# The idle products at the head of a fused attention and mixture kernel: strided, backward and narrower operands in place of shifted ones

## The chip, the cores and the metric

The kernel runs on one core of one Trainium2 chip. The metric is the device time of one execution in microseconds (us). The kernel before took 1054.14 us, the median of three runs (1053.22 to 1054.45). The profile was taken from one further execution.

## What is computed

The first half is a gated linear attention. For each of 4 batches and 8 heads (dimension 48) a 48 x 48 state runs over 768 positions; its output, with the heads laid side by side, is a 3072 x 384 matrix `x`. The second half sends `x` through four experts and adds them up, weighted by normalised probabilities.

```python
for t in range(S):
    state = alpha[:, :, t, :, None] * state + np.einsum('bhd,bhe->bhde', k[:, :, t], v[:, :, t])
    y[:, :, t] = np.einsum('bhd,bhde->bhe', q[:, :, t], state)
...
p = domain_probs / (domain_probs.sum(-1, keepdims=True) + 1e-09)
for e in range(E):
    h = np.maximum(x @ w1[e], 0.0)
    out += p[:, e:e + 1] * (h @ w2[e])
```

Here S = 768, E = 4, `w1[e]` is 384 x 1024 and `w2[e]` is 1024 x 384.

## The kernel before, in words

The sequence is cut into 24 units of 128 positions (6 blocks for each of 4 batches). `attention(u)` (L280) is a Python generator that issues one unit in 17 steps, so that other work can be issued between the steps. Its steps are, in order: transpose alpha (`tp`, L277) and copy it out as `AT` (ACT, L288); transpose k and copy it as `KT` (L293); transpose q and multiply it by `AT` into `QT` (DVE, L307). Then come seven levels: for each, ACT copies a half of `QT` into a block `qb` (L328), DVE multiplies `QT`, the decay `dec` and `KT` (L335, L337, L348), and the second half of `KT` is copied by POOL in unit 0 and by ACT in all others (L347). The scores of levels 0 to 3 are small products `sc` (L355) which DVE takes over into `near` under a mask (L365). Later `far` (L410) and the scores of levels 4 and 5 follow, then two steps that copy `far` and `near` into `lat` (L423, L428), then the unit's result `yps` (L450), which ACT copies out as a part of `xT` (L467), and last the state (`sps`, L489).

The experts work on groups of units. The first group holds units 0 and 1; the others hold four. `up` (L531) makes the hidden rows (`one` and `two`, L562 and L570) and `down` (L623) multiplies them with `w2` (`ops`, L663). `advance` issues attention steps of later units between these products, after a plan that is worked out from costs written in the program, not from the chip.

Everything is issued in program order on each engine's queue (`tc.manual_schedule()`), and each queue is worked off in that order.

The change lies in the head, before the first `up`. There the only work is the attention of unit 0 and a few steps of unit 1. Between its steps the program issues products whose operands are zeros and whose output `idle` nobody reads. There are two kinds:

- `fill(n)` (L796) issues n products of 128 x 128 zeros in plain float32, from a part of a state tile. Each is two pairs of weight load and product in the trace. Seven of them (14 pairs) open the PE queue.
- `single(n)` (L819) takes n entries from the list `turns` and issues four products of each, with `float32r` operands from the zeroed tile `nothing` (128 x 2304 words): one pair each. The stationary operand (`held`, the weight load) is 128 columns; the moving one is 384 words (two entries have 512).

An entry of `turns` before is told by how far the moving operand starts from word 640 (`away`), its width, the number of stationary columns (one entry has 96), and its form: plain, `one_line` (the same two words repeated 192 times), `one_word` for the stationary operand, or `backwards` (step -1). The list has 17 entries, 68 products. They are issued in list order, in six places of the PE queue: 4 after the transposes of alpha, 4 after those of k, 28 after those of q, 8 after the scores of levels 0 to 3, 8 after the transposes of unit 1's k, and 16 after the last scores, right ahead of `yps`. The third group of eight holds the entry with 96 columns and the `one_line` entry; the last 16 are `one_word`, the two entries of 512 words, and `backwards`, in that order.

In the loop at L828 a pair (u, n) says: issue the next step of unit u, then n entries.

```python
for u, n in ((0, 1), (0, 1), (0, 1), (0, 2), (0, 2), (0, 1), (0, 1), (1, 0), (0, 0), (0, 1),
             (0, 1), (1, 1), (0, 1), (1, 0), (0, 0), (0, 2), (0, 2), (0, 0)):
    next(runs[u])
    single(n)
```

Of the kernel before, what the change touches and what calls it, by code (L numbers as in the profile page):

```python
# [20 lines left out]
def kernel(  # L21
# [37 lines left out]
    nc = tc.nc  # L59

    B, H, S, D = q.shape
    E, DM, F = moe_w1.shape
    P = 128
# [3 lines left out]
    QUAD = 32  # L67
# [3 lines left out]
    NT = B * P  # L71
# [13 lines left out]
    n = np.arange(QUAD)[None, :]  # L85
# [81 lines left out]
    def load(u, names):  # L167
        if u >= len(units):
            return
        cb, b = units[u]  # L170
        for nm in names:
            src = srcs[nm][b, :, cb * P:(cb + 1) * P, :].rearrange("h s d -> s h d")
            if nm != "v":
                nc.sync.dma_start(out=raw(u, nm)[:, :, :D], in_=src)
                continue

            pairs = raw(u, nm).rearrange("p (a i) d -> p a i d", i=2)
            src = src.rearrange("p (a i) d -> p a i d", i=2)
            nc.sync.dma_start(out=pairs[:, :, 0, :D], in_=src[:, :, 0])
            nc.sync.dma_start(out=pairs[:, :, 1, :TAIL], in_=src[:, :, 1, QUAD:])  # L180
            nc.sync.dma_start(out=pairs[:, :, 1, TAIL:D], in_=src[:, :, 1, :QUAD])
# [13 lines left out]
    def load_piece(l, i, beside=False):  # L195
        if i >= E * NQ * LAST:
            return
        gi, k = divmod(i, E * NQ)
        e, c = divmod(k, NQ)
        if gi > l:  # L200
            w = wt[l][i] = wts.tile([P, 3, KC * QF], F32R, name=f"w{l + 1}",
                                    bufs=AHEAD if l == 0 else NQ)
            nc.sync.dma_start(out=w.bitcast(F32), in_=kept[l][k])
            return
        if l == 1 and not beside:
            return
        if l == 0:

            if gi > 0 or e == 0:
                shared[c] = wts.tile([P, 3, KC * QF], F32R, name="w2", bufs=NQ)  # L210
            w = shared[c][:, 2 - e % 2 if gi == 0 else 2].bitcast(F32)
        else:

            place = (hidden[c][:, 0] if not split2(gi, e, c) else hidden[c + NQ // 2][:, 1])
            w = place.rearrange("p f n -> p (f n)")[:, :KC * QF].bitcast(F32)
        wt[l][i] = w
        if l == 0:
            heads = moe_w1[e].rearrange("(h d) f -> h d f", d=D)[:, :, c * QF:(c + 1) * QF]
            w = w.rearrange("p (c f) -> p c f", f=QF)
            for part in range(2):  # L220
                nc.sync.dma_start(out=w[:, part], in_=heads[part * H // 2:(part + 1) * H // 2, :QUAD])
            nc.sync.dma_start(out=w[:, 2], in_=heads[:, QUAD:])
        else:
            nc.sync.dma_start(
                out=w.rearrange("p (c d) -> p c d", d=DM),
                in_=moe_w2[e].rearrange("(c p) d -> p c d", p=P)[:, c * FPQ:(c + 1) * FPQ])
# [36 lines left out]
    def norm_probs():  # L263
        nc.vector.reduce_sum(out=tot, in_=p_all, axis=AX.X)
        nc.vector.tensor_scalar_add(out=tot, in0=tot, scalar1=1e-9)
        nc.vector.reciprocal(out=tot, in_=tot)
        nc.vector.tensor_mul(p_all, p_all, tot.unsqueeze(2).broadcast_to([P, NBLK, E]))
        nc.vector.tensor_scalar_mul(out=p_fine, in0=p_all, scalar1=FINE)
# [439 lines left out]
    def cost(layer, gi, e):  # L708
        n = len(groups[gi]) / 4
        if layer == 0:  # L710
            return 2.1 * n if split1(gi, e) else 2.6 * n
        return 4.1 if gi > 1 else 4.7 if split2(gi, e) else 5.4
# [56 lines left out]
    with tc.manual_schedule():  # L769
        nc.scalar.dma_start(out=ident_all, in_=nc.inline_tensor(ident_np, name="ident_c").ap())  # L770
        nc.scalar.dma_start(out=masks, in_=nc.inline_tensor(mask_np, name="masks_c").ap())
        nc.gpsimd.memset(sts[B - 1], 0.0)
        for nm in "akq":
            for r in (early[nm], apart[nm]):
                nc.gpsimd.memset(r[:, :, D:], 0.0)
        nc.gpsimd.memset(lat[HALF:, :, :HALF], 0.0)
        for t in values + blocks:
            nc.gpsimd.memset(t, 0.0)
        for t in sts[:-1]:
            nc.gpsimd.memset(t, 0.0)  # L780

        load(0, "akqv")
        load(1, "akqv")
        nc.sync.dma_start(out=p_all, in_=moe_domain_probs.rearrange("(n p) e -> p n e", p=P))
        for i in range(NQ):
            load_piece(0, i)

        idle = ps.tile([P, NT], F32, name="idle", tag="g", bufs=4)  # L790
        zeros = sts[B - 1].rearrange("p a i d -> p (a i d)")[:, :P]
        nothing = wts.tile([P, 3, KC * QF], F32R, name="w1", bufs=AHEAD)
        nothing = nothing.rearrange("p t n -> p (t n)")
        nc.vector.memset(nothing.bitcast(F32), 0.0)

        def fill(n):  # L796
            for _ in range(n):
                nc.tensor.matmul(idle[:, :P], lhsT=zeros, rhs=zeros, start=True, stop=True)

        def words(n, at):  # L800
            return nothing[:, at:at + n]

        def one_line(n, at):
            return words(2, at).unsqueeze(1).broadcast_to([P, n // 2, 2])

        def one_word(n, at):
            return words(1, at).broadcast_to([P, n])

        def backwards(n, at):
            return words(n, at)[:, ::-1]  # L810

        def turn(away=16, n=DM, m=P, moving=words, held=words, pair=2):
            return away, n, m, moving, held, pair

        turns = deque([turn(), turn(0), turn(8), turn(24), turn(32), turn(40), turn(48), turn(56),
                       turn(4), turn(12), turn(pair=1), turn(m=3 * QUAD), turn(moving=one_line),
                       turn(held=one_word), turn(8, NT), turn(48, NT), turn(moving=backwards)])

        def single(n):  # L819
            for _ in range(n):  # L820
                away, n, m, moving, held, pair = turns.popleft()
                for i in range(4):
                    nc.tensor.matmul(idle[:m, :n], lhsT=held(m, 256 * (i % pair)),  # L823
                                     rhs=moving(n, 640 + away), start=True, stop=True)

        runs = [attention(u) for u in range(len(groups[0]))]
        fill(7)
        for u, n in ((0, 1), (0, 1), (0, 1), (0, 2), (0, 2), (0, 1), (0, 1), (1, 0), (0, 0), (0, 1),  # L828
                     (0, 1), (1, 1), (0, 1), (1, 0), (0, 0), (0, 2), (0, 2), (0, 0)):
            next(runs[u])  # L830
            single(n)
        norm_probs()

        span = cost(0, 0, 0) * FCH / 2 + cost(1, 0, 0)
        waiting.extend((span * (k + 1) / 15, u, runs[u])
                       for k, u in enumerate([1, 1, 1, 0, 1, 0, *[1] * 8]))
        for fc in range(FCH):
            up(0, 0, fc, slice(0, 1))
            advance(cost(0, 0, 0) / 2)
        down(0, 0, [0], deque())  # L840
        while waiting:
            next(waiting.popleft()[2], None)
        clock = 0.0
        waiting.extend((1.0 + k, 1, runs[1]) for k in range(2))
        waiting.extend(deal())

        for (gi, e), after in zip(tasks, [*tasks[1:], (None, None)]):
            rest = gi == e == 0
            for fc in range(FCH):
                up(gi, e, fc, slice(1, len(groups[0])) if rest else None)  # L850
                advance(cost(0, gi, e) / (2 if rest else 1))
            each = len(groups[gi]) if split2(gi, e) else 1
            turns = [range(k, k + each) for k in range(rest, len(groups[gi]), each)]
            for k, slots in enumerate(turns):

                between = deque()
                if after[1] == 0:

                    for step, at in enumerate((0.0, 0.3, 0.42, 0.54) if gi == 0 else
                                              (0.0, 0.6, 0.7, 0.78)):  # L860
                        at = at * len(turns) - k
                        if 0 <= at < 1:
                            between.append((at, lambda step=step: split_x(after[0], step)))
                down(gi, e, slots, between)
        while stores:
            stores.popleft()()
# [28 lines left out]
```

## Time and profile before

| | |
|---|---|
| median of three runs | 1054.14 us |
| the profiled execution: its own time | 1053.91 us |
| its span, first to last instruction | 1052.1 us |
| what lies around the span | 1.8 us |
| PE busy, share of the span | 98% |
| DVE, ACT, POOL busy | 74%, 54%, 4% |
| PE idle products at L823 | 68, from 5.0 to 24.2 us |
| PE idle products at L798 | 14, from 1.2 to 3.9 us |
| first instruction of `yps` (L450) | 24.48 us |
| first instruction of `one` (L562) | 26.16 us |

The page of the profile gives the busy time of each engine, the span in slices, the chain of work that ended last and the costliest groups of instructions. A row of a group reads: line, engine, operation, output and inputs, shapes, count, busy time and mean time of one. [...]

### The profile page before, as it was taken

Reading aid. Unit: us, or ns where it says so; the run is one execution under the profiler, and the core shown is the slowest. Engines: PE = TensorE matmul, PEld = TensorE weight load, DVE = VectorE, ACT = ScalarE, POOL = GpSimd, SP = SyncE. Lnnn points to the kernel's source line nnn. Section 1 sums busy time; section 2 is a strip of 40 time slices with the busy share of each in tenths; the row PEclk is TensorE's granted clock in tenths of the full one; section 3 lists DMA queues with packets and bytes.
Section 4 is the critical chain, followed back from the end, with each engine's and each line's share of the span. In section 5 each row is a group of like instructions: output and inputs, shape, how many; then the busy total and the mean of one; then the engine's idle time right before and its main releaser. Section 6 shows DMA issues by size and latency. Waiting matters only on the chain.

```text
span 1052.1 us, 21692 instructions
## 1 busy us (share of the span) xinstructions
PE 1035.5 (98%) x8538; PEld 900.9 (86%) x8538; DVE 780.7 (74%) x1621; ACT 566.3 (54%) x1195; POOL 37.8 (4%) x81
## 2 busy tenths in 40 slices
PE   9899999999999999999999999999999999999998
PEld 8776777687787898898898998898989989898998
DVE  6488777668779868778877777986877875656565
ACT  4687876675757545446455435555474443323232
POOL 3010010000000000000000000000000000000000
PEclk9999999999999999999999999999999999999999
DMA  7596799997967949669669569576594454444531
GB/s 117 165 324 204 250 308 342 324 343 230 314 249 256 381 148 328 257 211 313 231 212 329 193 231 360 184 275 253 169 366 181 181 210 178 183 182 178 206 154 45
DMA packets 158549, 251.66 MB, mean 239 GB/s; under 512 B 120144, under 2 KB 134864, under 8 KB 135920
## 3 DMA queue, kind: packets, MB, share of 16 engines
q1 hardware_dynamic: 151984, 207.89, 58.5%
q0 software_dynamic: 6016, 42.08, 10.0%
q8 instruction: 67, 1.10, 0.4%
q10 hardware_dynamic: 448, 0.32, 0.1%
q14 instruction: 34, 0.28, 0.1%
HBM read 207.79 MB, written 42.47 MB: 238 GB/s over the span
## 4 chain that ended last, share of the span: by engine, by line
PE 87%; DVE 6%; ACT 4%; DMA 1%; issue 1%; POOL 0%; SPq 0%; ACTq 0%; DVEq 0%; POOLq 0%
PE ops L663 35%; PE one L570 23%; PE two L570 11%; PE sc L355 6%; PE yps L450 3%; PE tp L277 3%; PE one L562 2%; ACT qb L328 1%; PE sps L489 1%; PE idle L823 1%; PE far L410 1%; DMA hT<-in_moe_w_dram 1%; DVE near L365 1%; DVE hT L616 1%; DVE acc L692 1%
## 5 line engine op out<-in xcount | busy, mean ns | idle before, releaser
L663 PE MATMUL ops<-w,hT 128*128 128x384 f32 x1872 | 342.7, 339 | 0.2 <-DVE hT L616 0.2
L663 PEld LDWEIGHTS ops<-w,hT 128*128 128x128 f32 x1872 | 322.6, 188 | 4.0 <-ACT t L581 0.7
L570 PE MATMUL one<-xT,w 128*128 128x512 f32 x960 | 251.8, 398 | 1.3 <-DVE QT L335 0.9
L570 PEld LDWEIGHTS one<-xT,w 128*128 128x128 f32 x960 | 176.1, 188 | 39.2 <-DVE QT L335 1.5
L581 ACT ACTIVATE t<-one 128x512 f32<-128x512 f32 (+1 forms) x192 | 107.0, 557 | 175.8 <-PE one L570 170.6
L328 ACT COPY qb<-QT 64x256 f32<-64x256 f32 x336 | 136.6, 406 | 58.6 <-DVE QT L335 30.4
L610 DVE SCALAR_TENSOR_TENSOR hT<-t,hT 128x512 fp32r<-128x512 f32 (+1 forms) x172 | 110.4, 642 | 63.3 <-ACT hT L608 62.4
L583 DVE TENSOR_TENSOR t<-t,two 128x512 f32<-128x512 f32 (+1 forms) x172 | 109.4, 636 | 53.2 <-PE two L570 32.0
L608 ACT ACTIVATE hT<-t 128x512 fp32r<-128x512 f32 (+1 forms) x172 | 101.8, 592 | 86.8 <-DVE t L583 86.2
L570 PE MATMUL two<-xT,w 128*128 128x512 f32 x480 | 136.4, 393 | 0.1
L570 PEld LDWEIGHTS two<-xT,w 128*128 128x128 f32 x480 | 90.0, 188 | 20.6 <-DVE acc L692 0.9
L663 PE MATMUL ops<-hT 128*128 128x384 f32 x288 | 100.8, 491 | 0.2
L616 DVE SCALAR_TENSOR_TENSOR hT<-hT 128x512 fp32r<-128x512 f32 (+1 forms) x172 | 100.6, 634 | 0.0
L365 DVE COPY_PREDICATED near<-masks,sc 128x256 f32<-128x256 uint8 x144 | 77.1, 535 | 22.3 <-PE sc L355 19.2
L335 DVE TENSOR_TENSOR QT<-QT,dec 128x256 f32<-128x256 f32 x144 | 61.0, 424 | 38.8 <-ACT qb L328 38.2
L355 PEld LDWEIGHTS sc<-qb,KT 128*64 128x64 f32 x2304 | 72.7, 138 | 9.0 <-issue 4.4
L355 PE MATMUL sc<-qb,KT 128*64 128x64 f32 x2304 | 77.2, 223 | 2.6 <-ACT qb L328 2.6
L663 PEld LDWEIGHTS ops<-hT 128*128 128x128 f32 x288 | 52.1, 190 | 30.1 <-DMA hT<-in_moe_w_dram 0.7
L692 DVE SCALAR_TENSOR_TENSOR acc<-ops,p_all,acc 128x384 f32<-128x384 f32 x82 | 49.8, 614 | 27.1 <-PE ops L663 26.3
L347 ACT COPY KT<-KT 128x256 f32<-128x256 f32 x138 | 57.5, 417 | 5.1 <-PE sc L355 1.9
L348 DVE TENSOR_TENSOR KT<-KT,dec 128x256 f32<-128x256 f32 x144 | 60.2, 418 | 0.0
L562 PE MATMUL one<-xT,w 128*128 128x256 f32 (+1 forms) x240 | 46.2, 340 | 0.6 <-ACT xT L467 0.6
(93 smaller groups left out, 939.5 us busy)
## 6 DMA issues: line engine op xcount, KB each, us to landing
w<-kept SPq DMA_DIRECT2D x144, 1152.0 KB
kept<-w POOLq DMA_DIRECT2D x32, 1152.0 KB, 7.3
hT<-in_moe_w_dram SPq DMA_DIRECT2D x32, 384.0 KB
w<-in_moe_w_dram SPq DMA_DIRECT2D x48, 128.0 KB
ra<-in_alpha_dram SPq DMA_DIRECT2D x23, 192.0 KB
rk<-in_k_dram SPq DMA_DIRECT2D x23, 192.0 KB
rq<-in_q_dram SPq DMA_DIRECT2D x23, 192.0 KB
out_dram<-acc POOLq DMA_DIRECT2D x22, 192.0 KB, 7.0
```

The lines of the kernel that those rows point to most:

```text
L328: nc.scalar.copy(out=qb[rows, :, i, :].rearrange("p a (b r) -> p a b r", r=m), in_=qv[rows])
L335: nc.vector.tensor_mul(qv, qv, spread(dv[:, :, :, 0], m))
L355: nc.tensor.matmul(out[HALF * s:HALF * (s + 1), 2 * p:2 * p + 2, :], lhsT=KTs[li][:, p, HALF * s:HALF * (s + 1)], rhs=qbs[li][:, p, :, QUA ...
L365: nc.vector.copy_predicated(near.rearrange("p a (b two r) -> p a b two r", two=2, r=m)[:, :, :, 1, :], mk.unsqueeze(1).broadcast_to([P, H, ...
L562: nc.tensor.matmul(one, lhsT=w[:, kc], rhs=xraws[gi][:, kc, lo:hi], start=(kc == 0), stop=(kc == KC - 1))
L570: nc.tensor.matmul(out, lhsT=w[:, part, kc], rhs=x_part(gi, part, kc), start=(part == terms[0] and kc == 0), stop=(part == terms[-1] and k ...
L581: nc.scalar.activation(out=t, in_=one, func=ACT.Copy, scale=FINE)
L583: nc.vector.tensor_add(t, t, two)
L608: nc.scalar.activation(out=top, in_=x, func=ACT.Relu, scale=TRIM)
L610: nc.vector.scalar_tensor_tensor(out=low, in0=x, scalar=0.0, in1=top.bitcast(F32), op0=ALU.max, op1=ALU.subtract)
L616: nc.vector.scalar_tensor_tensor(out=dif, in0=top.bitcast(F32), scalar=1 / 4096.0, in1=low.bitcast(F32), op0=ALU.mult, op1=ALU.subtract)
L663: nc.tensor.matmul(sums[at], lhsT=h, rhs=w, start=(n == begins[at]), stop=(n == ends[at]))
```

## The change

The list of entries is another one, and an entry is told by four numbers: the step between the stationary operand's columns (`held`: 1, 2, 3 or 4 words), the step between the moving operand's words (`moving`: 1, -1 or 2), the number of stationary columns (`m`: 128, once 66), and the offset `away`. All moving operands are 384 wide. There are 13 entries, and `single` issues six products of each instead of four: 78 products. In two places of the loop, after the transposes of alpha and of k, `fill(3)` stands now where `single(1)` stood; after the steps of levels 0 and 1 one entry is issued where there were two.

```diff
--- before.py
+++ after.py
@@ -800,35 +800,29 @@
         def words(n, at):
             return nothing[:, at:at + n]
 
-        def one_line(n, at):
-            return words(2, at).unsqueeze(1).broadcast_to([P, n // 2, 2])
-
-        def one_word(n, at):
-            return words(1, at).broadcast_to([P, n])
-
-        def backwards(n, at):
-            return words(n, at)[:, ::-1]
-
-        def turn(away=16, n=DM, m=P, moving=words, held=words, pair=2):
-            return away, n, m, moving, held, pair
-
-        turns = deque([turn(), turn(0), turn(8), turn(24), turn(32), turn(40), turn(48), turn(56),
-                       turn(4), turn(12), turn(pair=1), turn(m=3 * QUAD), turn(moving=one_line),
-                       turn(held=one_word), turn(8, NT), turn(48, NT), turn(moving=backwards)])
+        def turn(held=1, moving=1, m=P, away=16):
+            return held, moving, m, away
+
+        turns = deque([turn(), turn(2), turn(2, -1), turn(4), turn(4, -1), turn(m=66), turn(1, -1),
+                       turn(2, -1, away=12), turn(3), turn(3, -1), turn(1, 2), turn(1, away=20), turn(2, 2)])
+
+        def stepped(n, at, step):
+            span = words(n * abs(step), at)[:, ::abs(step)]
+            return span if step > 0 else span[:, ::-1]
 
         def single(n):
             for _ in range(n):
-                away, n, m, moving, held, pair = turns.popleft()
-                for i in range(4):
-                    nc.tensor.matmul(idle[:m, :n], lhsT=held(m, 256 * (i % pair)),
-                                     rhs=moving(n, 640 + away), start=True, stop=True)
+                held, moving, m, away = turns.popleft()
+                for i in range(6):
+                    nc.tensor.matmul(idle[:m, :DM], lhsT=stepped(m, 512 * (i % 2), held),
+                                     rhs=stepped(DM, 1024 + away, moving), start=True, stop=True)
 
         runs = [attention(u) for u in range(len(groups[0]))]
         fill(7)
-        for u, n in ((0, 1), (0, 1), (0, 1), (0, 2), (0, 2), (0, 1), (0, 1), (1, 0), (0, 0), (0, 1),
+        for u, n in ((0, 3), (0, 3), (0, 1), (0, 1), (0, 1), (0, 1), (0, 1), (1, 0), (0, 0), (0, 1),
                      (0, 1), (1, 1), (0, 1), (1, 0), (0, 0), (0, 2), (0, 2), (0, 0)):
             next(runs[u])
-            single(n)
+            (fill if n > 2 else single)(n)
         norm_probs()
 
         span = cost(0, 0, 0) * FCH / 2 + cost(1, 0, 0)
```

On the PE queue this gives, by place: 3 products of L798 (six pairs) where there were 4 of L823, twice; then 30 where there were 28; 12 where there were 8, of them six with 66 columns and six with a moving step of -1; 12 where there were 8 (`held` 2 with -1, `held` 3); and 24 where there were 16 (`held` 3 with -1, `moving` 2, plain at another offset, `held` 2 with `moving` 2). The first 30 are plain, `held` 2, `held` 2 with -1, `held` 4, and `held` 4 with -1. The queues of the other engines hold the same instructions in the same order as before.

## The prediction, as it was put on record

> **What bounds the kernel now.** I read the page first. PE is busy for 98% of the span and the chain of work that ended last is PE for 87%, so a microsecond added to the PE queue counts unless PE would have waited there anyway. The changed instructions all run before 25 us, so the second view is the chain of work over the first 34 us (start, length, what):
>
> ```profile
> 5.42 1.19 PE idle L823 x4
> 6.61 0.44 PE tp L277 x4
> 7.04 0.70 PE idle L823 x4
> 7.74 0.44 PE tp L277 x4
> 8.18 4.92 PE idle L823 x28
> 13.10 0.44 PE tp L277 x4
> 13.54 2.02 PE sc L355 x64
> 15.55 1.60 PE idle L823 x8
> 17.15 0.44 PE tp L277 x4
> 17.59 1.35 PE idle L823 x8
> 18.94 0.44 PE tp L277 x4
> 19.38 0.13 issue
> 19.50 0.66 PE far L410 x8
> 20.16 0.93 PE sc L355 x32
> 21.09 3.46 PE idle L823 x16
> 24.55 1.05 PE yps L450 x32
> ```
>
> From 5.42 to 25.60 us the pieces lie end to end on PE, with one gap of 0.13 us ahead of `far`. In this stretch the idle products themselves hold the queue: they take 4.92 + 1.60 + 1.35 + 3.46 = 11.33 us in the last four places. The third view, the timeline of DVE and ACT, asks whether anybody needs `yps` earlier:
>
> ```profile
> 22.39 0.43 DVE L428 COPY lat<-near 64x512 f32<-64x512 f32 x1
> ...
> 25.63 0.48 ACT L467 COPY xT<-yps 128x384 f32<-128x384 f32 x1 [2.92 <-PE yps L450]
> ```
>
> What `yps` reads (`lat`) is complete at 22.82 us, but `yps` starts at 24.48, because the last 16 idle products stand ahead of it. ACT has waited 2.92 us for it. So the length of the idle products is on the path already.
>
> **The price of one product.** From the x28 piece: 4.92 / 28 = 0.176 us for a plain one of 384 words. Of the x16 piece, 8 products have 512 words; the timeline of the piece gives 0.232 for one of these, and with 8 x 0.176 + 8 x 0.232 = 3.27 there is 0.19 left for the change over from the 64-column `sc` products. The x8 piece after `sc` shows the same: 1.60 - 8 x 0.176 = 0.19. The other x8 piece holds four products with 96 columns and the four that read one line: four at 0.174 and four at 0.165 make its 1.35. The backward moving operand stands last in the x16 piece, and its four products started 0.176 apart, as plain ones do: step -1 is free. In the after list it occurs in 30 products and costs nothing. The weight load with 96 columns is recorded 26 ns shorter than the one with 128 (162 against 188) while the product's distance stays at 0.174; so 66 columns save nothing, as the stream of 384 words sets the pace.
>
> **The sum without the steps.** By place of the PE queue:
> 1. After alpha: three plain float32 products (six pairs) for four of L823. In the trace a pair of L798 starts 0.213 us after the one before it, and one of L823 at that moment 0.320 us, since both still run at the slow clock (from 6.4 us on, the same pairs of L823 are 0.176 apart). 6 x 0.213 = 1.28 against 4 x 0.320 = 1.28: nothing.
> 2. After k: six pairs at the later clock. The nearest row is the same two-pair form in `one` (L562, 12 pieces in 1.34 us), 0.112 each, so 0.67 against 0.70: -0.03.
> 3. After q: 30 for 28: +0.35.
> 4. After `sc`: 12 x 0.176 + 0.19 = 2.30 against 1.60: +0.70.
> 5. After k of unit 1: 12 x 0.176 = 2.11 against 1.35: +0.76.
> 6. Ahead of `yps`: 24 x 0.176 + 0.19 = 4.41 against 3.46: +0.95.
>
> Together +2.73 us. The cover: `far` waits for ACT's last `qb`, which ends at 19.40. Between the transposes and `far` PE loses about 0.2 us (the gap of 0.13 and the overlap that `sc` shows in its place). In the changed kernel the k transposes of unit 1 end 1.0 us later (places 2 to 4), near 18.6. ACT's copy of them (L293), which began at 17.93 when ACT itself was free, now waits for PE, and the last `qb` ends near 20.1; but PE reaches `far` only at 21.1. The 0.2 are saved. So `yps` starts **2.5 us later**. DVE and ACT follow PE by then: the take-over of the last scores moves from 21.13 to about 22.7, `lat` to 24.4, the probabilities to 25.8, all before `yps` at 27.0. They stay hidden.
>
> **Does the delay reach the end?** ACT has `xT` (after `yps`) ahead of unit 1's `qb` copies in its queue, DVE's next work waits 4.68 us for these at 28.86, and `one` waits for `xT`. So PE, ACT and DVE all move together. What does not move are the loads that SP issues in the head; PE doesn't wait for them. The chain holds two waits for loads later on: one of v at 50.83 us (3.10), which SP issues after `sps`, and one of `w2` at 141.84 (11.52), which follows ACT's work; both are released by the work that is late, and for the second PE itself waits only 0.7 us. So I pass the delay on in full: 1053.91 + 2.5 = 1056.4.
>
> **The unknown: steps.** No PE row has a step of 2, 3 or 4. From below I allow nothing: a strided read cannot be quicker than a plain one by more than the one-line form showed (0.011 us a product, 0.1 us for the twelve). From above I use the quickest rate at which the trace shows PE reading: 384 words at 0.176 are 96 groups of four words, 1.8 ns a group. If a new group cannot be had faster, a moving step of 2 needs 192 groups, 0.35 us, +0.17 for 12 products: +2.1. For the stationary operand, a 128-column load passes in 0.109 (the transposes L277: 0.44 for 4), or 0.067 less than the stream that hides it. A step of 4 then needs 128 groups, 0.23, +0.06 for 12 products: +0.7. Steps of 2 and 3 need 64 and 96 groups, 0.12 and 0.18, and stay hidden. So the steps cost 0 to 2.8 us.
>
> DVE reads with a step of 2 (`dec` L337) at the same length as without, but it asks for a word only every 1.0 ns (L307 takes 0.68 us for 512 words, L335 0.42 for 256), where PE's stream takes one every 0.46. So this speaks only weakly for a free moving step of 2. Against it: one line 0.165, a plain stream 0.176, so changing groups is not quite free even at one in four words. I take the middle course: the moving step of 2 is free or nearly so, the stationary step of 4 (perhaps 3) costs about 0.04 for 12 products, +0.5. That gives 1053.91 + 3.0 = 1056.9, or **1057.0** against the median, which lies 0.23 above the profiled execution.
>
> [...]
>
> **Rivals.**
> - *No step costs anything*, since the load is hidden and the reads keep up: 1056.4 to 1056.6. For it: 0.067 us of cover on each load. Chance 0.22.
> - *The moving step of 2 halves the stream as well*: +2.1 +0.5 on 1056.4 gives 1059.0. For it: the one-line row. Chance 0.25.
> - *The head's delay is taken up* (not slower): between 26 and 52 us PE stands idle for about 5 us, waiting for unit 1's chain on ACT and DVE. If that chain began by itself, the 2.5 us would vanish there, and the time would be 1054. It decides if ACT's `qb` at 27.97 is not held by `xT` and the two `hT` copies ahead of it. Against it: ACT's queue is in order, and the chain shows ACT `hT` just before that `qb`. Chance 0.05.
> - *The steps are not what is read*, or the strided form breaks the stream and the clock falls to what the first products had (0.320 against 0.176): 78 x 0.144 = +11 us, about 1068. The products still follow each other without gaps, so I give it 0.03.
>
> **How the numbers follow.** The forecast, 1056.6 to 1057.4, has the remaining 0.45. About 0.2% (2.1 us) is what a measurement of this kernel can tell from no change: below 1052.0 is faster, above 1056.25 slower. Same takes the absorbed case and the lower edge of "no step costs" with the spread of medians: 0.15. Faster 0.02, for nothing here shortens the path. Slower 0.83. The range reaches from the lower bound less a little absorption, 1055.6, over the second rival to 1059.8 (the upper bounds 2.1 + 0.7 on 1056.4, with the median's offset and some spread).
>
> **What would show it.** In the profile after, `yps` should start at 27.0 plus the steps' cost, and `one` 1.7 later. The distances of the products with held 4 should be near 0.22, all others 0.176; a distance of 0.35 in the last 24 means the second rival; 0.176 throughout the first. The granted clock must stay full. It would be wrong if `yps` starts late and the end does not move.

## The result and the profile after

The changed kernel takes 1059.26 us, the median of four executions (1059.18 to 1059.36). The kernel before takes 1053.89 (four executions, 1053.22 to 1054.45). The ratio is 1.0051, with a 95% interval of 1.0034 to 1.0069: slower by 5.4 us. The span of the profiled execution went from 1052.1 to 1057.4 us, at a mean granted clock of 1.00. The forecast was slower, 1057.0, with a range of 1055.6 to 1059.8; the time came out where the second rival had put it (1059.0).

The chain of work over the head of the changed kernel, which answers to the one shown of before (start, length, what):

```profile
5.64 1.22 PE idle L798 x6
6.86 0.44 PE tp L277 x4
7.30 0.67 PE idle L798 x6
7.97 0.44 PE tp L277 x4
8.40 5.95 PE idle L817 x30
14.35 0.44 PE tp L277 x4
14.79 2.02 PE sc L355 x64
16.80 2.25 PE idle L817 x12
19.05 0.44 PE tp L277 x4
19.49 2.14 PE idle L817 x12
21.63 0.44 PE tp L277 x4
22.07 0.59 PE far L410 x8
22.65 0.93 PE sc L355 x32
23.58 6.52 PE idle L817 x24
30.10 1.05 PE yps L450 x32
```

The pieces still lie end to end, and the gap ahead of `far` is gone. Place by place against before: 5.95 for 4.92, 2.25 for 1.60, 2.14 for 1.35, and 6.52 for 3.46, together 5.53 us more. The two places with `fill` took 1.22 for 1.19 and 0.67 for 0.70. `yps` starts 5.55 us later than before (5.53, less 0.2 for the gap and a shorter `far`, and 0.2 because the first transposes took longer in this execution).

The timelines of ACT and DVE show who waits for it:

```profile
24.90 0.42 DVE L428 COPY lat<-near 64x512 f32<-64x512 f32 x1
...
31.18 0.48 ACT L467 COPY xT<-yps 128x384 f32<-128x384 f32 x1 [5.96 <-PE yps L450]
```

`lat` is complete at 25.32 us, 2.5 us later than before, since DVE and ACT now follow PE. The prediction had 24.4 without the steps; 0.7 of the stationary step of 4 and the 0.2 of the first transposes make up the rest. Yet `yps` comes only at 30.0, and ACT's wait has doubled from 2.92 to 5.96 us.

Which products are slow shows when the products of one entry are picked out by a window. A product's recorded time holds the distance to the next one and some 0.16 to 0.18 us more (a plain product: 338 ns recorded, 176 apart). Columns: minimum, median, maximum in ns. The first window lies around the entries with stationary step 4 (11.4 to 14.0 us, with two products of the entry before), the second around the one with stationary step 3, the third around the one with moving step 2:

```profile
L817 PE MATMUL idle<-w x14: 337/398/401, 11.0 to 14.0; 128*128 128x384 f32 x14
L817 PEld LDWEIGHTS idle<-w x12: 307/330/330, 11.2 to 13.8; 128*128 128x128 f32 x12
```
```profile
L817 PE MATMUL idle<-w x7: 339/341/348, 20.0 to 21.1; 128*128 128x384 f32 x7
L817 PEld LDWEIGHTS idle<-w x6: 250/252/257, 20.2 to 21.1; 128*128 128x128 f32 x6
```
```profile
L817 PE MATMUL idle<-w x7: 339/522/526, 24.6 to 26.4; 128*128 128x384 f32 x7
L817 PEld LDWEIGHTS idle<-w x7: 188/208/208, 24.6 to 26.4; 128*128 128x128 f32 x7
```

With stationary step 4 the loads are recorded at 330 instead of 188 ns and the products at 398; they start 0.234 us apart. With step 3 the loads take 252, but the products stay at 341: hidden. With moving step 2 the loads are nearly as before and the products take 522; they start 0.343 apart, twice the plain distance.

### The profile page after: what moved, and what is told of

Same layout as the page of the kernel before. It is cut to its first block, busy times and chain, and to the rows that moved or that the text cites. A ratio compares the mean times of both kernels' runs of the same rounds, so it can differ in the third digit from the quotient of the medians.

```text
span 1057.4 us, 21736 instructions
## 1 busy us (share of the span) xinstructions
PE 1041.3 (98%) x8560; PEld 905.3 (86%) x8560; DVE 780.9 (74%) x1621; ACT 565.7 (53%) x1195; POOL 37.7 (4%) x81
## 4 chain that ended last, share of the span: by engine, by line
PE 86%; DVE 5%; ACT 5%; DMA 2%; issue 1%; SPq 0%; POOL 0%; ACTq 0%; DVEq 0%; POOLq 0%
PE ops L663 35%; PE one L570 23%; PE two L570 11%; PE sc L355 6%; PE tp L277 3%; PE yps L450 3%; ACT qb L328 2%; PE idle L817 2%; PE one L562 2%; DMA hT<-in_moe_w_dram 1%; PE sps L489 1%; PE far L410 1%; DVE hT L616 1%; DVE near L365 1%; DMA rq<-in_q_dram 1%
```

## The experiments

All times below are medians, save those of the three kernels with other forms of operands (b1, b2, b3), which were executed once. Each is set against runs of the kernel before on the same chip. What is said of `yps` and of pieces comes from one profiled execution of each kernel.

**The moving step made plain.** The changed kernel with

```diff
-                       ... turn(3), turn(3, -1), turn(1, 2), turn(1, away=20), turn(2, 2)])
+                       ... turn(3), turn(3, -1), turn(), turn(1, away=20), turn(2)])
```

> The changed kernel (1059.26 us) with the two entries of moving step 2 read plainly (step 1); all else as changed. Theory A (a new group of four words cannot reach PE faster than one in 1.8 ns): the 12 products fall from 0.343 to 0.176 us, so 2.0 us less, about 1057.2, and yps starts 2.0 us earlier (near 28.0). Rival (the delay of the end comes from elsewhere, the clock's later rise and the loads behind it): within 0.5 us of 1059.3.

Measured: 1056.78 against 1053.58, ratio 1.0032 (1.0020 to 1.0044), so 3.2 us over the kernel before instead of 5.4. The piece ahead of `yps` is 2.1 us shorter than in the changed kernel, and the other three are the same:

```profile
7.93 5.95 PE idle L817 x30
...
16.33 2.25 PE idle L817 x12
...
19.02 2.14 PE idle L817 x12
...
23.11 4.44 PE idle L817 x24
```

`yps` started at 27.5 us, 2.55 earlier than in the changed kernel: 2.1 of that is this piece, and 0.5 lies at the first `fill` after the transposes of alpha, which took 0.74 us here and 1.22 there. Theory A holds for the size; the rival falls.

**The stationary step made plain.** `turn(4), turn(4, -1)` became `turn(), turn(1, -1)`.

> The changed kernel with the two entries of stationary step 4 read plainly (step 1). Theory A: a load of 128 groups takes 128 x 1.8 = 0.23 us and sticks out from under the stream; 12 products fall from 0.234 to 0.176, 0.7 us less, about 1058.6. Rival (the head has slack at this place, since ACT is ahead of the scores): no change, 1059.3.

Measured: 1058.70 against 1053.58, ratio 1.0048 (1.0035 to 1.0060). The x30 piece falls from 5.95 to 5.26 us, which is the 0.7 that was expected, the other three stay,

```profile
8.61 5.26 PE idle L817 x30
...
23.09 6.52 PE idle L817 x24
```

and the start of `yps` stands 0.5 earlier (5.06 instead of 5.55 late). The whole time fell by only 0.3 in the difference to before, which the interval cannot tell from 0.7 or from nothing. The price is shown at its place; at the end it isn't.

**All steps made plain.** Every 2, 3 and 4 made 1, so that the counts, the steps of -1 and the 66 columns are left.

> The changed kernel with every step of 2, 3 and 4 made 1; steps of -1, 66 columns, places and counts stay. Theory A: only the counts are left, 18 more products at 0.176 and 8 of them no longer 512 wide, +2.5 us on the kernel before (1053.9): about 1056.4 to 1056.6. Rival (the counts cost nothing because the head's delay is taken up later): about 1054.

Measured: 1056.07 against 1053.58, ratio 1.0021 (1.0013 to 1.0030): +2.5 us, the sum of the counts. The pieces:

```profile
7.97 5.26 PE idle L817 x30
...
15.68 2.24 PE idle L817 x12
...
18.36 2.11 PE idle L817 x12
...
22.42 4.38 PE idle L817 x24
```

The prediction had 4.92 + 0.35 = 5.27, then 2.30, 2.11 and 4.41 for these four. The rival (taken up later) falls.

**Ahead of `yps` nothing.** In the kernel before, the last two `(0, 2)` of the loop became `(0, 0)`; this leaves out the last 16 idle products.

> The kernel before without its last 16 idle products, those right ahead of yps. Theory B (yps waits only for these products, its inputs being complete at 22.8 us): yps starts near 22.9 instead of 24.5, 1.6 us less, about 1052.3. Rival (the products keep PE's clock up): the granted clock falls for a while and the time is 1054 or more.

Measured: 1052.58 against 1053.58, ratio 0.9992 (0.9983 to 1.0000). The median is 1.0 us less, at the edge of the interval. `yps` started 1.77 us earlier in the profiled execution, as theory B has it, but the windows of this execution show the fall of the clock that the rival spoke of (columns: PE, PEld, DVE, ACT, POOL busy, granted clock, DMA):

```profile
18.00:21.00 3.00, 2.61 (x48) 2.24 (x46) 2.85 (x9) 1.72 (x5) 0.00 (x0) 1.00 0.26 79
21.00:24.50 3.50, 1.21 (x33) 0.97 (x34) 2.58 (x9) 1.10 (x2) 0.00 (x0) 1.00 0.36 120
24.50:28.00 3.50, 3.50 (x17) 3.50 (x18) 0.00 (x0) 1.05 (x4) 0.00 (x0) 0.51 0.54 153
28.00:31.00 3.00, 3.00 (x29) 3.00 (x28) 2.07 (x6) 2.90 (x10) 0.00 (x0) 1.00 0.54 127
```

From 21 to 24.5 us PE was busy for 1.21 of 3.5 us. In the next 3.5 the granted clock is 0.51, and the first twelve products of `one` take 2.81 us, where they took 1.62 in the kernel before. Before and here:

```profile
26.16 1.62 PE one L562 x12
```
```profile
24.37 2.81 PE one L562 x12
```

Of the 1.77 us only 0.15 were left for `one` at 28 us, and 0.6 for ACT and DVE, and from 33 us on for all of the work. This execution took 1054.38 us, the longest of the eleven. In the other ten the mean granted clock was 0.999 or 1.000, and a stretch of 3.4 us at half clock (0.51 over 3.5 us) would take 0.0016 off it; so they had no such stretch. That the clock falls without the last idle products is shown once in eleven executions, and the median is that of executions without the fall. What sets off the fall, this one execution does not show.

**Fewer, but some.** To keep the clock and still be early, the last 16 became 8 plain ones (d1), and, in another kernel, none were left there and none after alpha and k (c1).

```diff
-        turns = deque([... turn(held=one_word), turn(8, NT), turn(48, NT), turn(moving=backwards)])
+        turns = deque([... turn(), turn()])
...
-                     ... (0, 2), (0, 2), (0, 0)):
+                     ... (0, 1), (0, 1), (0, 0)):
```

> The kernel before with 8 plain idle products of 384 words ahead of yps where there are 16 (these end near 22.6 us, as lat is complete at 22.8). Theory B with the clock kept up (the kernel without the 16 lost the clock at 24.6 us for 3.4 us and with it most of its 1.8 us): yps near 22.9 at full clock, 1.6 us less in the head, of which the first weights may take back up to 0.9; 1052.0 to 1052.8, the quickest so far. Rival (the clock's window falls all the same): as the kernel without the 16, some executions 1054.

> The kernel before without the last 16 idle products and without the four after alpha's and the four after k's transposes. Theory B (the idle products hold the queue in these places too; k's transposes began 1.0 us and q's 0.8 us after they could): the attention of unit 0 starts up to 0.8 us earlier and yps about 2 us earlier than in the kernel before, near 1052. Rival (PE now pauses between 5.4 and 8 us and the clock rises a stage later): unit 0's chain is not earlier, PE runs slow until about 10 us, and the time is 1052.5 to 1054.

Measured: d1 1052.79 against 1053.45, ratio 0.9995 (0.9986 to 1.0004); c1 1052.54 against 1053.47, ratio 0.9994 (0.9985 to 1.0003). Neither is told apart from the kernel before. In both profiled executions the clock stayed full once it had risen (the mean granted clock is 0.999, where a stretch like that of a4 gave 0.998), so neither rival's slow stretch came. `yps` started 1.62 us earlier in d1 and 2.02 in c1, as theory B has it in both. The chain of c1 shows a wait for weights:

```profile
21.55 8.61 DMA w<-in_moe_w_dram
30.15 0.04 issue
30.20 0.49 PE one L562 x2
```

These products of `one` stand only 0.4 to 0.7 us earlier than before. But this wait is not where the gain goes: behind these products PE had waited 1.1 us for ACT in the kernel before, and from 33 to 120 us the work stands 1.77 us early in c1 and 1.65 in d1. Most of it goes at later loads. At 137 us PE waits for a load of q in c1, where it did not wait before. Before, then c1:

```profile
137.37 0.60 PE L277 MATMUL tp<-ident,rq 128*128 128x128 f32 x4
```
```profile
136.77 0.63 PE L277 MATMUL tp<-ident,rq 128*128 128x128 f32 x4 [1.02 <-DMA rq<-in_q_dram]
```

Behind it d1 is 1.0 us early and c1 0.55. Near 164 us PE waits for weights from `kept`, in d1 for 1.7 us and in c1 for 0.9, while before it waited there for DVE for 0.9; from 200 us on 0.5 us are left in both. So in these executions the loads at 137 and 164 us take back most of what the head saves. The time of d1 lies at the upper end of what theory B had, that of c1 where its rival had it, though not for the rival's reason. No version beats the kernel before beyond the interval.

**Forms of the moving operand.** In two kernels, b1 and b3, the 13 entries of the changed kernel were replaced by other products of zeros. From b1:

```diff
+        def run(n, at, step=1, some=1, of=1):
+            span = words(n // some * of * abs(step), at)
+            if some < of:
+                return span.rearrange("p (a b) -> p a b", b=of)[:, :, :some]
...
```

> The changed kernel with other products of zeros in the 13 entries, all 384 wide, six each: plain; moving step 3; 4; 6; two words of each four; four of each eight; two of each eight, starting on a multiple of four words, and the same starting three words later; stationary step 8; plain float32 with moving step 1; 2; 4; moving step 2 from an odd word. Theory A (groups of four aligned words, 1.8 ns each): distances of 0.176; 0.52 (288 groups); 0.69 (384); 0.69; 0.34 (192); 0.176 (96); 0.34 (192); 0.69 (384, each pair lies across two groups); 0.234; float32 pairs 0.323; 0.34; 0.69; and 0.34. Rival (whatever is not a run of neighbours is read at half speed, whatever the step): 0.176; 0.34 for every step from 2 on; 0.34 for all pairs and fours.

> Other moving operands in the 13 entries, all of 384 words, six products each, stationary operand plain. Theory C (what counts is how many words are taken in a row from one aligned group of four: with one a group costs 0.88 ns, with two to four 1.76, with eight 3.4): plain 0.176; every eighth word twice 0.34; four of each eight 0.176; the same from one word later 0.25 (3 + 1), two later 0.34 (2 + 2), three later 0.25 (1 + 3); two of each eight from two later 0.34; every fourth word twice 0.34; every fourth word four times 0.176; each word twice 0.165; two of each four, the pair read twice, 0.176; eight of sixteen 0.176; six of each eight 0.225 (4 + 2). Rival (only a run of four or more neighbours goes at full speed, wherever it starts): 0.176 for four of eight from any start; 0.34 for every fourth word four times, each word twice, and the pair read twice.

Measured, as distances from start to start in the trace, 384 words each:

| words read by the moving operand | us |
|---|---|
| plain; four of each eight; eight of sixteen | 0.174 to 0.176 |
| step 2 (also from an odd word); step 3; 4; 6 | 0.340; 0.338; 0.347; 0.336 |
| two of each four; two of each eight, starting none, two, three words later | 0.340; 0.347; 0.346; 0.347 |
| four of each eight, starting one, two, three words later | 0.340; 0.340; 0.340 to 0.366 |
| six of each eight | 0.230 |
| every fourth word twice; every eighth word twice | 0.340; 0.346 |
| every fourth word four times; the pair of each four twice | 0.176; 0.177 |
| each word twice | 0.163 |
| plain float32, a pair (two pairs make a product): step 1; 2; 4 | 0.322; 0.338; 0.676 |

Theory A (1.8 ns for each group of four, however little is taken) holds for steps of 2, for pairs inside a group and for plain float32, and fails for steps of 3, 4 and 6 and for pairs across two groups: these were expected at 0.52 to 0.69 and took 0.34. The rival of that run fails by four of each eight, which were expected at 0.34 and took 0.175. Theory C, in b3, was right in eleven of the thirteen; the rows of four that start one and three words later failed (expected 0.25, measured 0.340 and up to 0.366). Its rival, that only the length of the run counts, falls on the same rows and on the words read four times (0.176, expected 0.34). What fits the float32r rows within 5%, but for two, is the lesser of two prices: 0.88 ns for each word read, or 1.77 ns for each aligned group touched. It was found after the fact and tried on no further form. The two are each word twice, which it would put at 0.085 and which took 0.163, 0.42 ns a word and the least of all rows; and some fours from three words later, at 0.366. So in these rows a stream of float32r words keeps its speed when four reads in a row fall in one aligned group (0.163 to 0.177), and is at half speed when two or fewer do (0.336 to 0.347). Three of the rows, from windows around step 4 (b1), around four of each eight one word later, and around each word twice (b3):

```profile
L824 PE MATMUL idle<-w x6: 530/531/532, 11.7 to 13.4; 128*128 128x384 f32 x6
```
```profile
L822 PE MATMUL idle<-w x8: 336/542/542, 11.4 to 13.5; 128*128 128x384 f32 x8
```
```profile
L822 PE MATMUL idle<-w x6: 326/326/430, 28.3 to 29.2; 128*128 128x384 f32 x6
```

The last two read neighbouring words; the runs of the first of them cross a group, the other stays in a group for eight reads.

The time of b1 was 1077.11 against 1053.47, and `yps` started 23.4 us late there: the end was 23.6 late. For b3 it was 1062.49 against 1053.45, 9.0 more, with `yps` 8.5 late.

**Forms of the stationary operand.**

> The changed kernel with other products in the 13 entries, six each: moving width 256 with stationary step 1, 2, 3, 4; width 512 with step 4; width 384 with step 4 and moving step 2; width 128 with stationary steps 1, 2, 3, 4; moving step 2 with widths 192 and 96; moving step -2 with 384. Theory A (a load passes at the longer of 0.107 us and 1.8 ns a group, and hides under the stream of the product ahead): distances 0.120; 0.12; 0.18; 0.234; 0.234 (under 0.229); 0.343 (hidden under the slow stream); 0.11; 0.12; 0.18; 0.234; 0.18; 0.11; 0.343. Rival (a stationary step costs a fixed time on top of the product, since loads and streams share the reading): 0.06 more than plain at step 4 for every width, so 0.18 at 256, 0.29 at 512 and 0.40 with the moving step of 2.

Measured distances: width 256 with stationary step 1, 2, 3, 4: 0.118, 0.118, 0.180, 0.235. Width 128: 0.112, 0.118, 0.175, 0.233. Width 512 with step 4: 0.235. Step 4 with moving step 2: 0.343. Moving step 2 with 192 and 96 words: 0.174 and 0.111; step -2: 0.350. Stationary step 8, in b1: 0.242 to 0.250. Theory A holds in every row of b2: with a load of step 4 the products start 0.233 to 0.235 us apart at 128, 256 and 512 words, and 0.234 at 384 in the changed kernel, so the load shows under 256 or 384 words and vanishes under a stream of 0.343. The rival (a fixed 0.06 on top) falls at 256 words, where it had 0.18, and at the moving step of 2, where it had 0.40. The line of step 4 under 256 words:

```profile
L824 PE MATMUL idle<-w x7: 342/396/403, 10.6 to 12.0; 128*128 128x256 f32 x7
```

In this run the clock fell too:

```profile
23.00:27.20 4.20, 4.20 (x38) 3.97 (x35) 2.83 (x9) 0.98 (x2) 0.00 (x0) 1.00 0.52 148
27.30:30.60 3.30, 3.30 (x37) 2.31 (x35) 0.00 (x0) 0.00 (x0) 0.00 (x0) 0.50 0.51 122
```

PE is shown as busy for all of the first window, and from 23.4 us on it held six products of 128 words, 0.233 us apart behind loads of step 4, six of 192 and six of 96 words with moving step 2, and then two of 384 with step -2. So here the clock fell to 0.50 behind a PE row that was full for 4.2 us. Whether it has to do with one of these products was not tried. The time was 1059.87 against 1053.47: `yps` started 4.3 us late, `one` 5.2 after the half clock, and the end came 6.4 late.

## Why the prediction was right, and where it was not

- *What bounds the head* was right: the idle products hold PE's queue up to `yps`. In all seven kernels that lengthened the head `yps` moved by the change in the last four pieces, within 0.6 us; the rest lies ahead of these pieces.
- *The counts* were right: +2.73 less 0.2 was worked out, and with all steps plain the pieces took 5.26, 2.24, 2.11 and 4.38, and the time rose by 2.5 us.
- *The fills* cost nothing, 1.22 for 1.19 and 0.67 for 0.70, as worked out. The slow clock that the prediction read from the distances there is borne out: the trace's record of the granted clock begins with its rise to 1.00, at 6.4 us before and at 6.7 in the changed kernel. *The cover* of 0.2 ahead of `far` was used up, as said.
- *Steps of -1 and 66 columns* were free: 0.176 and 0.174 apart.
- *The stationary step of 4* was put at 0.04 us a product and cost 0.058 (the upper end had 0.06); 0.7 us in place of 0.5. Steps of 2 and 3 stayed hidden (0.173 to 0.184 apart), as the upper bound had it.
- *The moving step of 2* is the step that failed: "the moving step of 2 is free or nearly so". It cost 0.167 us for each of 12 products, 2.0 us, the upper end of the range (0.17). The prediction had worked out this price from the 1.8 ns a group of the plain stream and then took the other end. That was an estimate of the author's which no PE row showed; the DVE row that reads one word per 1.0 ns speaks, by the prediction's own words, only weakly for it. The nearest row was PE's own: one line at 0.165, a plain stream at 0.176. It pointed the right way. That the time still fell inside the range is owed to its upper end. And the way to that price was in part luck: 1.8 ns for each group gives the right 0.34 at step 2, but 0.52 and 0.69 at steps of 3 and 4, which took 0.34 as well. That a group is four words no row had shown by then; b3 shows it: four of each eight take 0.175, and 0.340 from one word later.
- *Does the delay reach the end?* Nearly in full for the changed kernel: `yps` was 5.55 us late and the profiled execution 5.35. The table sets each kernel against the one before, in us; the first three columns are from the profiled executions, and b1, b2 and b3 have one execution only.

| | start of `yps` | work at 120 us | span | time |
|---|---|---|---|---|
| all steps plain (a3) | +2.25 | +2.27 | +2.5 | +2.5 |
| moving plain (a1) | +3.00 | +3.03 | +2.6 | +3.2 |
| stationary forms (b2) | +4.33 | +5.20 | +6.0 | +6.4 |
| stationary plain (a2) | +5.06 | +5.08 | +6.1 | +5.1 |
| changed | +5.55 | +5.54 | +5.3 | +5.4 |
| moving forms (b3; b1) | +8.52; +23.40 | +8.55; +23.37 | +8.6; +23.2 | +9.0; +23.6 |
| eight last (d1) | -1.62 | -1.66 | -0.5 | -0.7 |
| none last (a4) | -1.77 | -0.55 | +0.5 | -1.0 |
| none last, none after alpha and k (c1) | -2.02 | -1.79 | -0.5 | -0.9 |

Up to 120 us the shift is passed on as it is, but for the two executions in which the clock fell (a4, b2) and 0.2 us in c1, at its wait for weights. Nearly all that changes after that, from -0.6 to +1.2 us, changes between 137 and 180 us, where PE waits for loads of q, of `w2` and from `kept`.

For the changed kernel this has a place. At 138 us of before the delay grows to 5.9 us, with a wait for a load of q, and at 153 us to 6.23, with one for the load of `w2`; and then a wait is gone. From the lists of waits of PE, before and after:

```profile
PE one L570 <- DVE QT L335: 0.9, 1, 0.9
```
```profile
PE ops L663 <- DMA hT<-in_moe_w_dram: 0.4, 1, 0.4
```

While PE waits for the load, DVE catches up, and the wait of `one` for DVE at 165 us, 0.9 us in the kernel before, does not come up after. From there to the end the delay stays between 5.2 and 5.3.

What stays open: why a group that is touched once costs 0.88 ns in a stream with step 4 and twice that when three more words come from the next group; the end of the stationary step of 4, which was shown at its place but not in the time; and why the loads between 137 and 180 us land when they do.

## What to carry to other kernels

Price an added product by the distance from start to start in a row of like products, and see first what stands behind it in the queue. Here 18 extra zeros-by-zeros products cost 2.5 us in full, because `yps` waits only for them. A shorter head did not pay in the same way: of 1.6 to 2.0 us most went again at loads far behind it. A strided operand is priced against what it hides under: here a load with step 4 cost nothing under a stream of 0.343 us and 0.058 us under one of 0.176, while a moving operand of float32r words that reads an aligned group of four only once or twice doubled a product of 384 words at once (0.336 to 0.347 for 0.176). When two bounds are far apart, take the row of the engine itself over that of another engine.

## What was not expected of the hardware

- A run of four neighbouring words that starts off an aligned group of four is as slow (0.340 us) as a step of 2, and a moving step of 6 is no slower (0.336) than one of 2. In plain float32, a step of 2 is nearly free (0.338 against 0.322 for a pair) and one of 4 doubles it (0.676).
- The time at which the first products speed up differs from one execution to the next, though the first 14 pairs are the same: the granted clock first rises at 5.6 us with all steps plain and at 6.7 in the changed kernel, and over all eleven profiled executions between 4.1 and 7.4. So the six pairs of the first `fill(3)` took 0.67 us in the one, at 0.112 a pair, and 1.22 in the other, mostly at 0.213.
- Without the last 16 idle products the clock fell in one profiled execution: 3.5 us at 0.51, behind 1.21 us of work in the 3.5 before. Ten more of the same kernel show no such loss.
